# Converting weights beside a recurrence: more places for raw words, two pieces under way, fewer loads ahead of the inputs

## Chip, cores, metric

One core of one Trainium2 chip. The metric is device time in microseconds (us); the lower the better. Executions of one kernel within a round lie within about 0.5% of each other, so effects of a few tenths of a per cent need several runs and an interval; all runs here were in the fast state. Ratios are the mean time of one kernel's fast runs over that of the other's of the same rounds, so not quite the ratio of the medians that I quote. The experiments ran in other rounds than the result did: where two kernels of different rounds are compared, the ratios decide, and I give the difference that they make beside that of the medians.

## The reference, cut to what matters

```python
B, H, S, D = 4, 8, 768, 40
for t in range(S):                               # per batch and head, state is D x D
    y[:, :, t] = einsum('bhd,bhde->bhe', r_t, state)
    Sa = einsum('bhde,bhe->bhd', state, a_t)
    state = state * w_t[:, :, None, :] - outer(Sa, b_t) + outer(v_t, k_t)
x = y.transpose(0, 2, 1, 3).reshape(3072, 320)
h = x @ w_in                                     # 320 x 2048
out = (h * clip(h + 3, 0, 6) / 6) @ w_out        # 2048 x 320
```

The two weight matrices arrive as 64-bit floats. The kernel loads them as pairs of 32-bit words and makes 32-bit floats of them with its own operations, in 20 pieces of 512 KB.

## The kernel before

The recurrence is computed in blocks of 64 time steps. 24 units (a block of two batch entries' heads) are handled in groups of four. For each group a triangular matrix is inverted on VectorE (`fb` is its first operation, `tb` and `tt` its last two); a "third block" then completes the inverse with two small products on TensorE. Inverse and inputs feed the recurrence step of each unit (`U`, `UT`, `score`, `state`, `yg`), whose result `xt` feeds the two large products with `win` and `wout`.

The weight conversion is a Python generator. Each `next(weights)` puts one step of it into the instruction streams, between other work. In these traces each engine takes up its operations in the order of the program (in e1 below, VectorE stands in front of one of them until 46.09 us, and all that follows comes later), so where a step stands in the program decides what it can hold up.

```python
def raw_homes():             # where a piece's raw words land, and which piece must be done first
    ...                      # a, b: half of a free buffer each; c, d: in wout; e, f: in win
    order = [a, b, c, d, e, f, a, b, c, d, a, b, c, d, a, b, None, None, a, b]
    free = [None] * 6 + [0, 1, 2, 3, 6, 7, 8, 9, 10, 11, None, None, 14, 15]   # None: fb, tt

for _ in range(4):           # four loads at once, on SP's queue, ahead of V and of the next inputs
    load()
yield
while n < PIECES + 2:        # three pieces under way (begun, not finished): n, n-1, n-2
    # piece n:    exponent:  VectorE shift/and -> parts, then ScalarE scales parts     | step
    # piece n-1:  sign:      VectorE or's the sign into parts                          | step
    #             mantissa:  VectorE and/or on raw, then ScalarE scales raw            | step
    # piece n-2:  combine:   VectorE raw = lo * 2**-52 + raw                           | step
    #             product:   VectorE out = raw * parts; done; load what may be loaded  | step
```

```python
for t, _ in enumerate(by_twos(0, 4, MIXED, 0, {5: 1, 6: 1, 10: 1})):   # prepare 4 units
    ...                      # conversion steps at t = 5, 6 and 10: six by then
while not third:             # the inversion: one conversion step for every third of its steps
    ...
while phase[0] in (3, 4):    # finish the piece's combine and product
    next(weights)
firsts = [third_block(*third[-1], n, True) for n in (0, 2)]
run(firsts[0])
next(firsts[1])              # the second block's first product, sent ahead
run(firsts[0], weight=1)
...
for t in range(LAST + OWN):  # the first group's recurrence, 2.5 conversion steps a TensorE stage
    if t in (1, 3): run(firsts[1])
    ...
```

```python
def third_block(F, tb, tt, n, others=False):
    ...                                            # 32 small products into zp
    for x in range(2): nc.scalar.activation(out=zs[...], in_=zp[x][...])      # 32x512 each
    if others:
        for z in range(0, P, BL):
            nc.scalar.activation(out=tinv[z:z + L, heads, 0:L], in_=tb[...])
            nc.gpsimd.tensor_copy(tinv[z + L:z + BL, heads, L:BL], tb[...])
    ...                                            # 32 small products into tp
    for x in range(2): nc.scalar.activation(out=tinv[..., L:BL], in_=tp[x][...])
```

## Time and profile before

| | before |
|---|---|
| time, median | 864.86 us (864.53 to 865.4, 4 runs) |
| span of the profiled run | 863.8 us, mean TensorE clock 0.926 |
| TensorE busy | 781 us, 90% of the span |
| VectorE busy | 530 us, 61% |
| ScalarE, GpSimd busy | 312 us, 150 us |

The lines behind this are in the prediction below. TensorE is full from about 160 us on. Everything that the change touches lies before that. So I follow a few marks through all the kernels: the start of `fb` (the inversion may begin), the start of `tb` (it ends), the first U product (the recurrence begins), and the first scan of the second group (`prods`, after which only work follows that no kernel here changes, save the last conversions).

### The profile page before, as it was taken

The page shows a single profiled execution, that of the slowest core. Times are in us where ns is not written, and L with a number is a line of the kernel's source. Part 1 is how long each engine was busy: PE and PEld are TensorE (multiplying, and loading weights), DVE is VectorE, ACT ScalarE, POOL GpSimd, SP SyncE. Part 2 cuts the span into 40 slices and gives each one's busy share as a digit, 9 for nine tenths or more (in the row PEclk, how much of TensorE's full clock was granted, in tenths as well). Part 3 has the DMA queues.
Part 4 walks back from the last instruction along what each step waited for, and adds up shares of the span by engine and source line. Part 5 has one row for each costly group of instructions (what it writes and reads, how often), then busy time and mean ns, then how long its engine had stood idle before and what let it go on. Part 6 is the DMA issues. An engine that isn't in the chain of part 4 may idle for free.

```text
span 863.8 us, 34857 instructions
## 1 busy us (share of the span) xinstructions
PE 781.1 (90%) x15480; PEld 668.2 (77%) x15480; DVE 529.6 (61%) x1032; ACT 311.9 (36%) x752; POOL 150.2 (17%) x295
## 2 busy tenths in 40 slices
PE   4541787898999999999999999999999999999998
PEld 3441766687888787888888888888888888888886
DVE  6689777967954669845589643698445774221211
ACT  1223744232344443344423534325453324222211
POOL 4220210122112130311130222112112201000000
PEclk8565657898999998999999999999999999999999
DMA  7733263431033331322321333222132101100000
GB/s 150 147 69 88 52 163 84 79 56 34 16 57 55 55 60 27 55 44 41 54 49 31 58 55 52 41 51 37 37 60 43 26 18 27 28 20 14 15 19 16
DMA packets 174326, 45.00 MB, mean 52 GB/s; under 512 B 157408, under 2 KB 172768, under 8 KB 174176
## 3 DMA queue, kind: packets, MB, share of 16 engines
q1 hardware_dynamic: 165632, 41.46, 24.9%
q10 hardware_dynamic: 8544, 1.31, 1.0%
q8 instruction: 122, 2.00, 1.0%
q14 instruction: 28, 0.23, 0.1%
HBM read 34.08 MB, written 3.93 MB: 44 GB/s over the span
## 4 chain that ended last, share of the span: by engine, by line
PE 77%; DVE 10%; DMA 5%; issue 3%; SPq 2%; ACT 1%; POOL 1%; ACTq 0%; DVEq 0%
PE o L936 24%; PE h L912 20%; PE any L418 6%; PE h L917 6%; PE any L436 3%; PE any L809 3%; PE any L832 3%; PE any L656 2%; SPq L404 2%; DVE prod L624 2%; DVE x L630 2%; DMA raw<-in_moe_w_in_dram 1%; PE any L716 1%; PE any L754 1%; PE any L581 1%
## 5 line engine op out<-in xcount | busy, mean ns | idle before, releaser
L936 PE MATMUL o<-wout,gt 128*128 128x320 f32 x768 | 232.5, 449 | 0.0
L912 PE MATMUL h<-xt,win 128*128 128x128 f32 x1536 | 197.3, 283 | 3.7 <-DVE gt L923 3.7
L912 PEld LDWEIGHTS h<-xt,win 128*128 128x128 f32 x1536 | 186.0, 196 | 11.7 <-DVE gt L923 3.8
L936 PEld LDWEIGHTS o<-wout,gt 128*128 128x128 f32 x768 | 141.2, 192 | 55.7 <-issue 2.4
L923 DVE SCALAR_TENSOR_TENSOR gt<-gt,h 128x512 f32<-128x512 f32 x96 | 61.3, 679 | 98.2 <-ACT gt L922 98.1
L922 ACT ACTIVATE gt<-h,three 128x512 f32<-128x512 f32 x96 | 60.6, 683 | 132.4 <-PE h L917 128.7
L847 POOL TENSOR_TENSOR yg<-ys,gam 128x512 f32<-128x512 f32 x24 | 41.7, 1736 | 234.8 <-DVE ys L844 123.0
L624 DVE TENSOR_TENSOR prod<-x 128x30 f32<-128x30 f32 (+9 forms) x180 | 65.6, 365 | 13.6 <-POOL x L615 8.1
L630 DVE TENSOR_TENSOR x<-x,prod 128x30 f32<-128x30 f32 (+9 forms) x180 | 64.5, 358 | 5.7 <-DMA R<-in_r_dram 0.4
L554 POOL TENSOR_TENSOR KBt<-K,rgt 128x320 f32<-128x320 f32 x24 | 21.6, 898 | 211.2 <-ACT rgt L546 211.2
L917 PE MATMUL h<-xt,win 64*128 64x128 f32 x768 | 55.8, 285 | 0.0
L445 DVE COPY_PREDICATED score<-mask,any 128x256 f32<-128x256 int32 x143 | 53.0, 433 | 3.2 <-PE any L436 3.2
L917 PEld LDWEIGHTS h<-xt,win 64*128 64x128 f32 x768 | 46.6, 187 | 4.5 <-issue 0.3
L472 DVE RECIPROCAL gam<-prods 128x256 f32<-128x256 f32 x24 | 41.4, 1740 | 13.5 <-POOL yg L847 13.2
L844 DVE TENSOR_TENSOR ys<-any,ys 128x256 f32<-128x256 f32 x44 | 16.6, 418 | 49.6 <-PE any L581 32.4
L487 DVE RECIPROCAL rgam<-prods 128x256 f32<-128x256 f32 x24 | 41.8, 1740 | 0.0
L461 DVE TENSOR_TENSOR_SCAN prods<-wm,start 128x528 f32<-128x528 f32 x24 | 30.0, 1252 | 17.0 <-ACT wm L458 15.4
L695 ACT ACTIVATE RT<-any 128x512 f32<-128x512 f32 x24 | 14.3, 595 | 71.6 <-PE any L418 71.5
L816 DVE TENSOR_TENSOR state<-any,state 128x160 f32<-128x160 f32 x48 | 13.2, 315 | 44.0 <-PE any L436 40.1
L587 ACT ACTIVATE EV<-any 64x160 f32<-64x160 f32 x92 | 24.8, 295 | 36.2 <-PE any L581 22.0
L832 PE MATMUL any<-score,KBt 64*64 64x64 f32 x1536 | 30.2, 229 | 1.7 <-DVE RR L721 1.4
L832 PEld LDWEIGHTS any<-score,KBt 64*64 64x64 f32 x1536 | 26.6, 142 | 6.5 <-issue 3.7
(159 smaller groups left out, 1144.1 us busy)
## 6 DMA issues: line engine op xcount, KB each, us to landing
V<-in_v_dram SPq DMA_DIRECT2D x96, 40.0 KB
out_dram<-ob SPq DMA_DIRECT2D x48, 80.0 KB
B<-in_b_dram SPq DMA_DIRECT2D x46, 80.0 KB
K<-in_k_dram SPq DMA_DIRECT2D x46, 80.0 KB
R<-in_r_dram SPq DMA_DIRECT2D x84, 40.0 KB
W<-in_w_dram SPq DMA_DIRECT2D x40, 80.0 KB
A<-in_a_dram SPq DMA_DIRECT2D x40, 80.0 KB
raw<-in_moe_w_out_dram SPq DMA_DIRECT2D x6, 512.0 KB
```

Of the source, the lines that this page charges most:

```text
L418: nc.tensor.transpose(out=o[:, n, :], in_=x[:, 2 * n:2 * n + 2, :].rearrange("p s e -> p (s e)"), identity=ident[:])
L445: nc.vector.copy_predicated(out=x[:, 4 * i:4 * i + 4, :], mask=mask4, data=o[i])
L487: nc.vector.reciprocal(rv[:, :, HB:BL], o["prods"][:, :, 1, 1:HB + 1])
L624: nc.vector.tensor_tensor(out=pv, in0=_ap(x[:], (i + 1) * L + i, [[L, n], [0, i]]), in1=_ap(x[:], i * L, [[0, n], [1, i]]), op=ALU.mult,)
L630: nc.vector.tensor_tensor(out=rest, in0=rest, in1=pv, op=ALU.add)
L832: nc.tensor.matmul(out=y[q][half(s), pr, :], lhsT=o[name][half(q), h * D:h * D + SLOT], rhs=m[name][half(q), 4 * rs + 2 * s + j, :], start ...
L847: nc.gpsimd.tensor_tensor(out=yg[:], in0=m["ys"][:].rearrange("p r q t -> p r (q t)"), in1=o["G"][:], op=ALU.mult)
L912: nc.tensor.matmul(out=hp[c][:, i, :], lhsT=win[:, t, j * P:(j + 1) * P], rhs=xt[:, t, :], start=(t == 0 and i == 0), stop=False)
L917: nc.tensor.matmul(out=hp[c][:, i, :], lhsT=win2[half(c), (j0 + i) * P:(j0 + i + 1) * P], rhs=xt[half(c), 2, :], start=False, stop=(i == N ...
L922: nc.scalar.activation(out=gt[:], in_=hp[c][:], func=AF.Relu, bias=three[:], scale=1.0)
L923: nc.vector.scalar_tensor_tensor(out=gt[:], in0=gt[:], scalar=6.0, in1=hp[c][:], op0=ALU.min, op1=ALU.mult)
L936: nc.tensor.matmul(out=op[:], lhsT=gts[c][:, n, :], rhs=wout[:, c * HJ + r * NQ + n, :], start=((split or r == 0) and c == 0 and n == 0), ...
```

## The change

Its intent: let inputs pass ahead of weights at the start; let weight loads run further ahead later, by three more places; give a place back sooner by having two pieces under way; let the first unit's recurrence begin when its own half of the inverse is there.

```diff
-        order = [a, b, c, d, e, f, a, b, c, d, a, b, c, d, a, b, None, None, a, b]
-        free = [None] * 6 + [0, 1, 2, 3, 6, 7, 8, 9, 10, 11, None, None, 14, 15]
+        order = [a, b, c, d, e, f, a, b, c, d, a, b, "fb", "tt", "x", d, a, b, "fb", "tt"]
+        free = [None] * 6 + [0, 1, 2, 3, 6, 7, None, None, None, 9, 10, 11, 12, 13]
...                                                   # load(): stops at limit[0], 2 at first
-        for _ in range(4):
-            load()
+        while load():
+            pass
...                                                   # the loop, two pieces under way:
-        # n: exponent | n-1: sign | n-1: mantissa | n-2: combine | n-2: product
+        # n: exponent | n-1: combine | n-1: product | n: sign | n: mantissa
...                                                   # in the preparation's loop:
+        limit[0] = {7: 4, 10: 12}.get(t, limit[0])
+        while t == 7 and refill[0]():
+            pass
...
-    while phase[0] in (3, 4):
+    while phase[0] in (1, 2, 3):
...
-    next(firsts[1])
...                                                   # in the recurrence's loop:
+        if t == 3:
+            limit[0] = PIECES
...                                                   # third_block, for the first blocks:
+        parts = [slice(0, H), slice(H, 2 * H)] if first else [slice(0, 2 * H)]
...          # every copy once per part; tb's copies on ScalarE go to GpSimd
```

More of the change, by code (lines that the diff above doesn't have):

```diff
@@ L224 @@
     phase = [0]
+    limit, refill = [2], []
     def raw_homes():
@@ L238, in raw_homes @@
         a, b, c, d, e, f = places
-        order = [a, b, c, d, e, f, a, b, c, d, a, b, c, d, a, b, None, None, a, b]
-        free = [None] * 6 + [0, 1, 2, 3, 6, 7, 8, 9, 10, 11, None, None, 14, 15]
+        order = [a, b, c, d, e, f, a, b, c, d, a, b, "fb", "tt", "x", d, a, b, "fb", "tt"]
+        free = [None] * 6 + [0, 1, 2, 3, 6, 7, None, None, None, 9, 10, 11, 12, 13]
+        left = {}
         for n, (x, before) in enumerate(zip(order, free)):
-            if x is None:
-                x = inv.tile([P, L, L], F32, name=f"raw{n}", tag=("fb", "tt")[n % 2])
-                x = x[:].rearrange("p t s -> p (t s)").bitcast(U32)
+            if isinstance(x, str):
+                if x not in left:
+                    left[x] = inv.tile([P, L, L], F32, name=f"raw_{x}", tag=x)
+                x = left[x][:].rearrange("p t s -> p (t s)").bitcast(U32)
                 x = x.rearrange("p (n c t) -> p n c t", n=2, t=2)
@@ L258, in load @@
         def load():
+            if issued[0] == min(PIECES, limit[0]):
+                return False
             if not upcoming:
-                if issued[0] == PIECES:
-                    return False
                 upcoming.append(next(homes))
@@ L272, in load @@
             return True
-        for _ in range(4):
-            load()
+        while load():
+            pass
+        refill.append(load)
         phase[0] = 0
         yield
-        stages = deque([None, None])
-        n = 0
-        while n < PIECES + 2:
+        before = None
+        for n in range(PIECES + 1):
             now = None
             if n < PIECES:
-                if not loaded:
-                    load()
+                while load():
+                    pass
                 out, raw = loaded.popleft()
+                hi = raw[:, :, :, 1]
                 x = ffn.tile([P, 2, WC], U32, name="parts", tag="gt", bufs=5)
-                now = n, out, raw, x
-                nc.vector.tensor_scalar(x[:], raw[:, :, :, 1], 20, 0x7FF, ALU.logical_shift_right,
+                now = out, raw, x
+                nc.vector.tensor_scalar(x[:], hi, 20, 0x7FF, ALU.logical_shift_right,
                                         ALU.bitwise_and)
                 nc.scalar.activation(out=x[:], in_=x[:], func=AF.Relu, bias=low[:], scale=2.0 ** 23)
-                if n < 2:
-                    load()
                 phase[0] = 1
                 yield
-            stages.append(now)
-            if stages[1]:
-                _, out, raw, x = stages[1]
-                hi = raw[:, :, :, 1]
+            if before:
+                out, raw, y = before
+                m, yf = raw[:, :, :, 1].bitcast(F32), y[:].bitcast(F32)
+                nc.vector.scalar_tensor_tensor(m, raw[:, :, :, 0], 2.0 ** -52, m, ALU.mult, ALU.add)
+                phase[0] = 2
+                yield
+                if len(out.shape) == 4:
+                    m, yf = (z.rearrange("p n (j c) -> p n j c", c=out.shape[3]) for z in (m, yf))
+                nc.vector.tensor_tensor(out=out, in0=m, in1=yf, op=ALU.mult)
+                converted[0] += 1
+                done.append(n - 1)
+                while load():
+                    pass
+                phase[0] = 3
+                yield
+            if now:
                 nc.vector.scalar_tensor_tensor(x[:], hi, 0x80000000, x[:], ALU.bitwise_and,
                                                ALU.bitwise_or)
-                phase[0] = 2
+                phase[0] = 4
                 yield
@@ L305, in load_weights @@
                                         ALU.bitwise_or)
-                hi = hi.bitcast(F32)
-                nc.scalar.activation(out=hi, in_=hi, func=AF.Copy, bias=-7.0, scale=2.0 ** -20)
-                phase[0] = 3
-                yield
-            if stages[0]:
-                k, out, raw, x = stages[0]
-                hi = raw[:, :, :, 1].bitcast(F32)
-                nc.vector.scalar_tensor_tensor(hi, raw[:, :, :, 0], 2.0 ** -52, hi, ALU.mult, ALU.add)
-                phase[0] = 4
-                yield
-                m, xf = hi, x[:].bitcast(F32)
-                if len(out.shape) == 3 and out.shape[1] != 2:
-                    m, xf = (y.rearrange("p n (j c) -> p (n j) c", c=out.shape[2]) for y in (m, xf))
-                elif len(out.shape) == 4:
-                    m, xf = (y.rearrange("p n (j c) -> p n j c", c=out.shape[3]) for y in (m, xf))
-                nc.vector.tensor_tensor(out=out, in0=m, in1=xf, op=ALU.mult)
-                converted[0] += 1
-                done.append(k)
-                while load():
-                    pass
+                m = hi.bitcast(F32)
+                nc.scalar.activation(out=m, in_=m, func=AF.Copy, bias=-7.0, scale=2.0 ** -20)
                 phase[0] = 5
                 yield
-            stages.popleft()
-            n += 1
+            before = now
     def weight_pieces():
@@ L647, in invert, with third_block @@
         yield
-    def third_block(F, tb, tt, n, others=False):
-        heads = slice(n * H, (n + 2) * H)
+    def third_block(F, tb, tt, n, first=False):
         zs = tmp.tile([P, 2 * H, L], F32, name="zs")
+        parts = [slice(0, H), slice(H, 2 * H)] if first else [slice(0, 2 * H)]
         zp = [ps_any([P, 2 * H, L]) for _ in range(2)]
@@ L659, in third_block @@
         yield PE
-        for x in range(2):
-            z = x * BL
-            nc.scalar.activation(out=zs[z:z + L], in_=zp[x][z:z + L], func=AF.Copy)
-        if others:
-            for z in range(0, P, BL):
-                nc.scalar.activation(out=tinv[z:z + L, heads, 0:L], in_=tb[z:z + L, heads],
-                                     func=AF.Copy)
-                nc.gpsimd.tensor_copy(tinv[z + L:z + BL, heads, L:BL], tb[z + L:z + BL, heads])
+        for part in parts:
+            for x in range(2):
+                z = x * BL
+                nc.scalar.activation(out=zs[z:z + L, part], in_=zp[x][z:z + L, part], func=AF.Copy)
+        if first:
+            for part in parts:
+                heads = slice(n * H + part.start, n * H + part.stop)
+                for z in range(0, P, BL):
+                    nc.gpsimd.tensor_copy(tinv[z:z + L, heads, 0:L], tb[z:z + L, heads])
+                    nc.gpsimd.tensor_copy(tinv[z + L:z + BL, heads, L:BL], tb[z + L:z + BL, heads])
         yield DONE
@@ L676, in third_block @@
         yield PE
-        for x in range(2):
-            z = x * BL
-            nc.scalar.activation(out=tinv[z:z + L, heads, L:BL], in_=tp[x][z:z + L], func=AF.Copy)
+        for part in parts:
+            heads = slice(n * H + part.start, n * H + part.stop)
+            for x in range(2):
+                z = x * BL
+                nc.scalar.activation(out=tinv[z:z + L, heads, L:BL], in_=tp[x][z:z + L, part],
+                                     func=AF.Copy)
         yield DONE
@@ L1040 @@
             next(weights)
+        limit[0] = {7: 4, 10: 12}.get(t, limit[0])
+        while t == 7 and refill[0]():
+            pass
         if t == RFETCH:
```

## The prediction

> **What bounds the kernel now.** I read four views, in this order: the page's slices, the waits of VectorE from 0 to 48 us with the timeline there, the waits of VectorE from 87 to 160 us, and the chain of work that ended last. The slices show where there is still time to gain.
>
> ```profile
> PE   4541787898999999999999999999999999999998
> ...
> DVE  6689777967954669845589643698445774221211
> ...
> PEclk8565657898999998999999999999999999999999
> DMA  7733263431033331322321333222132101100000
> ```
>
> A slice is 21.6 us. From the eighth or ninth on (about 160 us) TensorE is at 8 or 9 tenths and its clock near full: from there a fixed amount of matmul work sets the end. Only before that are there large gaps, and there the whole diff acts. So I take it that the end moves by what the start gets shorter, and ask what sets the start. It has three stretches: **A**, four units are prepared until their inversion can begin (0 to 47 us); **B**, the inversion on VectorE with weight conversions between its steps (47 to 87 us); **C**, the first recurrence steps with the rest of the conversions (87 to about 155 us, the last conversion ends at 155.5).
>
> Stretch A: VectorE's waits (total us, times, longest us), then two lines of the timeline.
>
> ```profile
> DVE bt L496 <- PE h L418: 6.5, 2, 3.6
> ...
> DVE fb L612 <- ACT F L516: 1.3, 1, 1.3
> ```
> ```profile
> 37.34 1.08 PE L418 MATMUL h<-ident,B 128*128 128x128 f32 x4 [2.42 <-DMA B<-in_b_dram]
> ...
> 41.62 1.09 PE L418 MATMUL h<-ident,B 128*128 128x128 f32 x4 [3.20 <-DMA B<-in_b_dram]
> ```
>
> VectorE waits 6.5 us for two transposes, and the transposes wait for the B input of the third and fourth unit. VectorE is otherwise busy nearly all the time from 14 us to 35.6 us. So the inputs of the second pair come late by 6.5 us, and then B begins (fb, 47.35 us). The next view says why they are late: the order of issue on the SP queue.
>
> ```profile
> 13.22 2.02 SPq L270 DMA_DIRECT2D raw<-in_moe_w_in_dram  x4
> 15.28 1.82 SPq L270 DMA_DIRECT2D wout<-in_moe_w_in_dram  x4
> 18.18 8.33 SPq L401 DMA_DIRECT2D V<-in_v_dram  x8
> ...
> 30.66 2.04 SPq L270 DMA_DIRECT2D win<-in_moe_w_in_dram  x4
> 32.81 1.28 SPq L404 DMA_DIRECT2D B<-in_b_dram  x2
> ...
> 36.21 1.14 SPq L270 DMA_DIRECT2D win<-in_moe_w_out_dram  x2
> 37.44 1.28 SPq L404 DMA_DIRECT2D B<-in_b_dram  x2
> ```
>
> Six weight pieces of 512 KB are issued before the second B. V's eight issues took 8.33 us here and 5.25 us at 40 us, so the queue also pushed back behind the weights.
>
> Stretch C: VectorE's waits from 87 to 160 us, and what the chain that ended last has there (start us, us, what).
>
> ```profile
> DVE parts L288 <- DMA raw<-in_moe_w_in_dram: 3.6, 2, 2.1
> DVE parts L288 <- DMA raw<-in_moe_w_out_dram: 3.1, 2, 2.4
> ...
> DVE parts L288 <- DMA wout<-in_moe_w_in_dram: 1.4, 1, 1.4
> ```
> ```profile
> 100.28 5.16 DMA raw<-in_moe_w_in_dram
> ...
> 109.63 4.45 DMA wout<-in_moe_w_in_dram
> ...
> 119.48 2.77 DMA raw<-in_moe_w_in_dram
> ...
> 122.51 5.09 DMA raw<-in_moe_w_out_dram
> ...
> 135.61 3.94 DMA raw<-in_moe_w_out_dram
> ```
>
> The chain goes through five weight loads, 21.4 us together; VectorE stands still for 8.1 us of that, and since it works in program order, the recurrence's own operations stand behind it. The loop is: a piece is done, its place is free, the next load starts, four to five us later the load lands, the conversion that was already due goes on.
>
> **What the Trainium skill says.** "DMA: Bandwidth & Descriptors", section "Issuing engines are not separate DMA queues": all issuers share the same 16 DMA engines and interleave. The trace agrees: 79% DMA share from 20 to 40 us, and V slowed behind weights. The same page, "Rules for kernel authors": issue a DMA early and wait for it late, so that its cost lies beside compute. The five loads above break that, with up to 5.2 us each from issue to landing on the chain. "GPSIMD Engine Reference", "Engine selection": one-input elementwise work runs about at line rate there. Here the 32x512 copies (L667) took 605 to 1043 ns on GpSimd and 627 ns on ScalarE (L665): agreement at best, worse beside VectorE. "TensorE: Matmul & The Clock Gate", "What's actually happening": recent activity releases the clock. The trace agrees in sense: 0.50 to 0.62 from 60 to 140 us, 1.00 in most of what follows 160 us.
>
> **The change part by part.**
>
> 1. *Fewer loads ahead of the inputs.* The limit is 2 pieces until step 7 of the preparation, so four of the six pieces leave the queue ahead of the second B. Issue time saved: 1.82 + 2.04 + 1.14 = 5.0 us, and V's push-back, 8.33 - 5.25 = 3.1 us if it all goes. The second B's issue moves from 37.4 to about 30 us, the first's to the moment its buffer is free (KBt's copies end at 27.4 and 29.1 us). Landing 4.2 to 4.5 us after issue as now, they are there at 32 and 34 to 35 us, before VectorE is through with its own work at 35.6. The 6.5 us go. Cost: the first sign operation now follows its own exponent directly, with ScalarE's 0.72 us between; the wait of 0.5 us there becomes about 1.0. And before the inversion two conversion operations of 0.68 replace 0.42 + 0.68, but a ScalarE operation of 0.72 ahead of F's copies goes. Sum for A: 6.5 - 0.5 + 0.5, so **6.5 us** sooner.
>
> 2. *Stretch B.* The number of conversion steps between inversion steps is unchanged, and so are their operations (0.42, 0.68, 0.42, 0.68, 0.68 us a piece). Piece 2 is now first read at the ninth step instead of the fifth, about 8 us into B; its load, issued near 40 us, should be there. **0 us.**
>
> 3. *More places, two pieces under way.* Counting conversion steps in the code (five a piece, 2.5 per TensorE stage in C): piece k was done at step 5k+9 and is done at 5k+6; piece n was first read at step 5n-5 and is at 5n-1. What matters is the distance from a place's release to the read of the piece loaded into it. Before, from piece 10 on, the place came from piece n-4 (save 16 and 17): 5n-11 to 5n-5, six steps, a little over one piece's time, and with SP's own issues ahead of it the load of 4 to 5 us is not covered. Afterwards pieces 12 to 14 take places that no conversion has to release (fb, tt, x, free once the first third blocks are through), the later ones come from piece n-6: 5n-24 to 5n-1, 23 steps. Pieces 10 and 11 keep n-4, but now that is 13 steps. So all five chain loads leave the chain. No VectorE operation is added. VectorE's 8.1 us of waiting are the direct worth. Its whole idle time from 87 to 155 us is some 15 us, 3.9 of it on the state's matmuls and 2.4 on gt, which stay. In place of the DMA the recurrence's own TensorE and ScalarE waits should take a little: I count 85% of 8.1, **7 us**. The conversions fall as exponent with combine, then product, sign and mantissa, 2.5 steps per TensorE stage, so ScalarE's results have a stage between them and their reader; I charge nothing for the shorter pipeline.
>
> 4. *Third blocks by unit.* Two ScalarE copies of tb (1.27 us) per block go to GpSimd, in eight halves, at an estimated 0.4 to 0.6 us each; they need only tb (ready 87.1) and so end about 91.5, ahead of the last product. zs and the last copies are halved: four of about 0.37 in place of two of 0.59. The product can begin after two of them, the first unit's U after two more: about 0.4 us at each of two places, **1 us**.
>
> Sum 6.5 + 0 + 7 + 1 = 14.5 us. I take off 10% for what is lost on the way to the end, 13 us: **852 us**.
>
> **The rivals.**
>
> *The recurrence takes over in C.* TensorE's own waits from 87 to 160 us are for state (3.9 us), gt (3.7) and ScalarE (about 4). If the weights only hid these, the 7 become 2 and the time is 857. Against it: the chain stays with the conversions and their loads nearly without a break from 98 to 140 us.
>
> *The loads collide later.* About 2 MB move from before 40 us to after it, onto V, A and R of the second pair. If piece 2 or the last inputs come late, B begins its conversions with a stall, some 2 to 4 us: 855. For it: 92 GB/s are moved there already. Against it: the first DMA waits of the conversions come only after 100 us.
>
> *A warmer clock pays more.* With no DMA stalls in C TensorE is denser, and its clock may rise before 150 us. TensorE's 42 us of busy time from 87 to 140 at 0.5 to 0.7 would shrink; a part of it on the chain gives 3 to 5 us more: 847 to 849.
>
> *Nothing arrives at the end.* If the later gaps were spare time that absorbs a shift, the time stays near 862. Against it: after 160 us TensorE waits about 7 us in total up to 220 us, and none of that is for the weights.
>
> **Range and chances.** The first two rivals together make 857 to 858, the third 846 to 848. Range 846 to 858. Two per cent faster means under 847.8, which needs the third rival or the whole of C's idle time: 0.22. Slower by two per cent has no mechanism: 0.01.
>
> **What would show it.** In the profile after: no TensorE wait on B near 40 us, and fb beginning near 41 us instead of 47.35 (step 1); tb 38 us after fb, as now (step 2); no VectorE wait of parts on a weight DMA between 87 and 155 us, the chain free of weight loads, and the last product about 14 us earlier, near 141 (step 3); the first U about 5 us after tb's end instead of 6 (step 4). The prediction is wrong if fb does not move, if the DMA waits turn into waits of parts or raw on ScalarE, or if the last product comes 14 us sooner and the end does not.

## The result

| | before | after |
|---|---|---|
| time, median | 864.86 us | 860.60 us (859.18 to 860.94, 4 runs) |
| ratio | | 0.9947, 95% interval 0.993 to 0.9964 |
| span of the profiled run | 863.8 us | 859.2 us |
| TensorE / VectorE busy | 781.1 / 529.6 us | 779.3 / 531.6 us |

Faster by 0.5%, where 1.5% was forecast. The marks tell where it went (us; from one profile each. The changed kernel, e7, e8 and e10 below have the same program up to `fb` and begin it between 39.93 and 40.66, so up to 0.7 us is noise):

| mark | before | after | lead | forecast lead |
|---|---|---|---|---|
| fb begins | 47.35 | 39.93 | 7.4 | 6.5 |
| tb begins | 85.20 | 78.40 | 6.8 | 6.5 |
| first U product | 93.18 | 85.58 | 7.6 | 7.5 |
| first scan, second group | 155.42 | 149.25 | 6.2 | 14.5 |
| end | 863.8 | 859.2 | 4.6 | 13 |

Up to the first U the forecast holds. Then the lead was to double, and it shrank. The page's slices of the changed kernel:

```profile
PE   4723877898999989999999999999999999999998
...
PEclk8755667998999999999999999999999999999999
DMA  7571452331123230322222233222132101100000
```

TensorE's slices two to six differ from those before; from the seventh on it is nearly the old picture. The SP queue of the changed kernel (start us, us, instruction), to be held against the seven lines of before:

```profile
13.22 2.03 SPq L273 DMA_DIRECT2D raw<-in_moe_w_in_dram  x4
15.29 6.68 SPq L396 DMA_DIRECT2D V<-in_v_dram  x8
...
27.04 2.06 SPq L399 DMA_DIRECT2D B<-in_b_dram  x2
...
30.57 1.27 SPq L399 DMA_DIRECT2D B<-in_b_dram  x2
```

Two weight pieces in place of six stand ahead of the second B, which is issued at 30.6 instead of 37.4 us. VectorE's wait of 6.5 us for `bt` is gone; its work then runs without a gap into `fb` at 39.93. A wait of 1.3 us of `fb` on ScalarE's copies of F went too, since the conversion's operation ahead of them did. This part did what it was meant to do.

Now VectorE's waits of the changed kernel from 87 to 160 us (total us, times, longest us):

```profile
DVE parts L313 <- ACT parts L294: 5.3, 3, 2.2
DVE raw L300 <- ACT raw L321: 2.7, 3, 1.9
DVE prods L456 <- ACT wm L453: 2.6, 2, 1.8
...
DVE raw_fb L300 <- ACT raw_fb L321: 0.8, 2, 0.4
...
DVE wout L300 <- ACT wout L321: 0.4, 1, 0.4
```

No wait for a weight load is left in this view, where there were 8.1 us. In their place stand 5.3 + 2.7 + 0.8 + 0.4 = 9.2 us in which VectorE waits for ScalarE's two conversion operations, and before there were none. (Counted from its own tb, 78.40 us, one more such wait belongs to the changed kernel, 1.9 us at 84.67 us: 11.1 us in all.) One new wait took the place of another. The largest single one, on both engines' timelines:

```profile
103.05 0.60 ACTq L396 DMA_DIRECT2D R<-in_r_dram  x1
103.61 0.57 ACT L697 ACTIVATE RT<-any 128x512 f32<-128x512 f32 x1
103.69 3.24 ACTq L396 DMA_DIRECT2D R<-in_r_dram  x3
106.98 0.72 ACT L294 ACTIVATE parts<-parts,low 128x512 uint32<-128x512 uint32 x1 [2.79 <-DMA raw_x<-in_moe_w_in_dram]
```
```profile
103.32 0.42 DVE L292 TENSOR_SCALAR parts<-raw 128x512 uint32<-128x512 uint32 x1
...
107.73 0.69 DVE L313 SCALAR_TENSOR_TENSOR parts<-raw,parts 128x512 uint32<-128x512 uint32 x1 [2.23 <-ACT parts L294]
```

VectorE had the exponent ready at 103.74. ScalarE came to it at 106.98, since it stood in its own queue's four issues of R from 103.05 to 106.93 (one operation, RT, ran beside the first). The bracket in ScalarE's line blames the load of `raw_x` for 2.79 us, but VectorE reads that piece only at 119.67 us; e7 will test the queue. It was held while the weights were being loaded at the same time (82% DMA share and 204 GB/s moved from 100 to 113 us). VectorE, with only combine and product between the exponent and the sign, then waited. In the kernel before, the same four issues held ScalarE from 109.62 to 112.34 us, and its list has no wait of `parts` or `raw` on ScalarE.

So the theory that I took into the experiments: **with two pieces under way VectorE has no slack against a ScalarE that is held by something else.** The rival is the prediction's own: the recurrence's chain takes over once the loads are gone, whatever the pipeline.

### The profile page after: what moved, and what is told of

Same layout as the page of the kernel before. It is cut to its first block, busy times and chain, and to the rows that moved or that the text cites. A ratio compares the mean times of both kernels' runs of the same rounds, so it can differ in the third digit from the quotient of the medians.

```text
span 859.2 us, 34883 instructions
## 1 busy us (share of the span) xinstructions
PE 779.3 (91%) x15480; PEld 665.8 (77%) x15480; DVE 531.6 (62%) x1032; ACT 311.3 (36%) x756; POOL 157.3 (18%) x307
## 4 chain that ended last, share of the span: by engine, by line
PE 75%; DVE 14%; issue 3%; ACT 3%; DMA 3%; SPq 2%; POOL 0%; ACTq 0%; DVEq 0%
PE o L938 23%; PE h L914 19%; PE any L413 6%; PE h L919 5%; PE any L431 3%; PE any L811 3%; DVE x L625 2%; DVE prod L619 2%; PE any L834 2%; PE any L653 2%; PE any L672 2%; PE any L756 1%; SPq L399 1%; PE any L576 1%; PE any L718 1%
## 5 line engine op out<-in xcount | busy, mean ns | idle before, releaser
L619 DVE TENSOR_TENSOR prod<-x 128x30 f32<-128x30 f32 (+9 forms) x180 | 65.7, 365 | 13.6 <-POOL x L610 8.1
```

The costliest lines, as they stand in the source:

```text
L619: nc.vector.tensor_tensor(out=pv, in0=_ap(x[:], (i + 1) * L + i, [[L, n], [0, i]]), in1=_ap(x[:], i * L, [[0, n], [1, i]]), op=ALU.mult,)
```

## The experiments

"C" is the length from tb to the first scan, "tail" from that scan to the end of the span, both from each run's profile. Times are medians, ratios against the kernel before in the same rounds.

| run | time us | ratio (95%) | fb | C | tail |
|---|---|---|---|---|---|
| before | 864.86 | | 47.35 | 70.2 | 708.4 |
| after | 860.60 | 0.9947 (0.993 to 0.9964) | 39.93 | 70.9 | 710.0 |
| e1 inputs first alone | 867.12 | 1.0022 (1.0015 to 1.003) | 48.39 | 71.7 | 708.9 |
| e2 places alone | 859.69 | 0.994 (0.9927 to 0.9952) | 47.18 | 65.1 | 707.8 |
| e3 third blocks alone | 865.85 | 1.0011 (1.0002 to 1.0019) | 46.77 | 71.4 | 708.0 |
| e4 after, three pieces | 863.47 | 0.9978 (0.997 to 0.9986) | 48.82 | 65.8 | 709.0 |
| e5 e4, loads after step 5 | 855.21 | 0.9889 (0.9874 to 0.9904) | 41.26 | 66.7 | 708.4 |
| e6 e5, old third blocks | 854.13 | 0.9876 (0.9862 to 0.989) | 40.85 | 65.7 | 707.9 |
| e7 after, issues off ScalarE | 856.71 | 0.9908 (0.9895 to 0.9922) | 40.38 | 66.7 | 710.3 |
| e8 after, one piece ahead | 859.05 | 0.9936 (0.9923 to 0.9948) | 40.66 | 69.3 | 708.5 |
| e9 e6, issues off ScalarE | 853.61 | 0.9865 (0.9847 to 0.9884) | 40.82 | 65.6 | 708.5 |
| e10 e7 and e8 | 856.21 | 0.989 (0.9873 to 0.9907) | 40.22 | 67.0 | 708.1 |

### First four: each part alone, and the pipeline undone

**e1**, in the kernel before: `limit` and `refill` as in the change, with {7: 4, 10: PIECES}; nothing else.

> The kernel before with one part alone: two weight pieces ahead of the inputs, two more after step 7, the rest from step 10; places, three pieces under way and third blocks as before. Theory (the inputs' gain is whole and reaches the end): fb begins near 40 us instead of 47.35, the first U near 86, and the time is 7 us under before, 857 to 858.5. Rival (the moved loads come back as waits in the conversions after 87 us): fb as early, but the DMA waits of parts grow from 8.1 to 11 us or more and the time is 861 to 863.

Both theories failed: 867.12 us, slower than before. `fb` came no sooner (48.39 us). Its VectorE waits from 0 to 48 us say why:

```profile
DVE parts L290 <- DMA wout<-in_moe_w_in_dram: 8.4, 1, 8.4
```

The inputs did come early. But with three pieces under way, piece 2 is read at the fifth conversion step, which stands in the program ahead of `fb`. Its load was now issued after step 7 of the preparation, at 40.5 us. VectorE sat in front of that one operation until 46.09, and everything behind it, `fb` included, came later than in the kernel before. In the change the same load is harmless because two pieces under way put that read off to the ninth step, behind `fb`. So as it is written, the first part of the change pays only together with the two pieces under way.

**e2**, in the kernel before:

```diff
-        order = [..., a, b, c, d, a, b, None, None, a, b]
+        order = [..., a, b, "fb", "tt", "x", d, a, b, "fb", "tt"]     # and free, as in the change
+    limit = [12] until t == 3 of the recurrence                       # fb, tt are free from there
```

> The kernel before with one part alone: the new order of places (fb, tt, x for pieces 12 to 14), three pieces under way, four loads ahead as before. Theory (weight loads set stretch C, and what ate the gain is the shorter pipeline): the DMA waits of parts from 87 to 160 us fall from 8.1 to under 3 us and the time falls by 4 to 7 us, 858 to 861. Rival (the recurrence's own chain sets stretch C, the loads only hid it): the DMA waits fall as much, waits on other engines take their place, and the time stays within 1.5 us of before.

859.69 us, as the theory had it, and about what the whole change brings (the intervals overlap). C is 5.1 us shorter. The waits of VectorE from 87 to 160 us, where before has 8.1 us on weight loads:

```profile
DVE parts L291 <- DMA raw<-in_moe_w_in_dram: 1.1, 1, 1.1
...
DVE parts L291 <- DMA raw_fb<-in_moe_w_out_dram: 0.2, 1, 0.2
```

6.8 us of waiting removed, 5.1 us of C gained: a quarter is lost to something else, and that is the most that the prediction's rival can claim. What takes that quarter was not tested.

**e3**, in the kernel before: `third_block` as in the change, `next(firsts[1])` taken out.

> The kernel before with one part alone: third blocks copied by unit, tb's copies on GpSimd, the second block's first product no longer sent ahead. Theory (in the changed kernel the lead on before fell from 7.6 us at the first U to 5.1 us at the first score after it, where the second block's product now stands among the recurrence): the first U comes 0.5 to 1 us sooner, the first score 1 to 2 us later, the time is 1 to 2 us over before. Rival (the prediction's): 1 us under before.

865.85 us, 0.1% slower. From tb's start the first U comes after 7.2 us instead of 8.0, the gain that I forecast at 1 us. But the first score after it comes 16.7 us after tb instead of 15.0, and C as a whole is 1.2 us longer. The second block's first product now stands among the recurrence's own stages; that this is the cause is likely, not shown, since e3 changes the copies as well.

**e4**, in the changed kernel: the loop of the kernel before, `while phase[0] in (3, 4)`.

> The changed kernel with three pieces under way again, all else as changed. Theory (VectorE's 9.2 us of waits on ScalarE's parts and raw from 87 to 160 us are what the shorter pipeline costs): those waits fall under 3 us and the time falls 3 to 6 us, to 855 to 858. Rival (the recurrence's own chain takes over whatever the pipeline): the waits fall but the time stays within 1.5 us of the changed kernel's 860.6.

863.47 us, slower than the changed kernel, so both stated ranges failed, and the reason is that of e1: its wait of `parts` on `wout` before `fb` is 8.3 us, and `fb` comes at 48.82. But C, the stretch in dispute, is 65.8 us against 70.9: 5.0 us shorter with three pieces, and VectorE waits for ScalarE's `parts` or `raw` nowhere in it. The theory was right for C, and I had not thought of what three pieces do before `fb`.

### Second four: getting both gains

**e5**, in e4:

```diff
-        limit[0] = {7: 4, 10: 12}.get(t, limit[0])
-        while t == 7 and refill[0]():
+        limit[0] = {5: 4, 10: 12}.get(t, limit[0])
+        while t == 5 and refill[0]():
```

> The changed kernel with three pieces under way, and pieces 2 and 3 loaded after step 5 of the preparation instead of step 7, that is directly behind the inputs of the second pair. Theory (the inputs' gain was lost in e1 and e4 only because, with three pieces, piece 2 is read before fb and its load stood behind V; it is a matter of that one load): the 8.3 us wait of parts on wout falls under 1 us, fb begins near 40 us, stretch C keeps e4's length, and the time is 7 to 9 us under e4's 863.5, 854 to 857. Rival (two pieces are needed for the inputs' gain, the load comes too late in any place after the inputs): the wait stays at 4 us or more, the time is 859 to 861.

855.21 us. The loads of pieces 2 and 3 now stand directly behind the second pair's inputs and ahead of V. The 8.3 us became

```profile
DVE parts L292 <- DMA wout<-in_moe_w_in_dram: 0.5, 1, 0.5
```

and `fb` begins at 41.26, with C still short: 66.7 us, 4.2 under the changed kernel. As e5 starts as early as that kernel does and e4 does not, 4.2 us is the fairer price of two pieces in C. They are not needed for the inputs' gain.

**e6**, in e5: `third_block` and `next(firsts[1])` as before the change.

> e5 with the third blocks as before the change, so the kernel before with only inputs first, places and the load after step 5. Theory (third blocks by unit cost about 1 us, as e3 says): 1 us under e5, 853 to 856, which beats both kernels by 4 us or more. Rival (they gain once C is not held by loads): 1 us over e5.

854.13 us, 1.1 us under e5, so third blocks by unit cost about a microsecond here too, with the loads out of the way (the intervals of e5 and e6 overlap; e3's lies wholly above 1, and both point the same way). This version keeps two of the change's four parts, with one load moved, and beats both kernels: 1.2% under before, 0.7% under after.

**e7**, in the changed kernel:

```diff
-            fetch("R", i + 1, nc.scalar if i < NU - 1 else None)
+            fetch("R", i + 1)                       # SP's queue
...
-                fetch(name, NU + 1, nc.scalar)      # W, A of unit 5
+                fetch(name, NU + 1)
```

> The changed kernel with R of units 1 to 3 and W and A of unit 5 issued from SP instead of ScalarE's queue. Theory (with two pieces under way VectorE waits for ScalarE because ScalarE's own DMA issues hold it, 3.8 us near 103 and 3.7 us near 131): the waits of parts and raw on ScalarE from 87 to 160 us fall from 9.2 to about 5 us and the time falls 3 to 4 us, to 857. Rival (it is the short distance itself, one VectorE operation between ScalarE's copy and its reader): the waits fall by under 1.5 us, the time stays within 1 us of 860.6 or grows because R comes later.

856.71 us: the theory's number (3.9 us by the medians, 3.4 by the ratios; the intervals are apart). The first of VectorE's waits after 87 us is cut from 5.3 us to

```profile
DVE parts L313 <- ACT parts L294: 1.2, 1, 1.2
```

while `raw` on ScalarE stays at 2.7; all waits on ScalarE's conversions from 87 to 160 us fall from 9.2 to 5.1 us. C is 66.7 us, 4.1 shorter, the same as that of e5. No operation changed, only the queue from which five small groups of input loads are issued. So of the 4.2 to 5.0 us that two pieces cost in C (against e5 or e4), 4.1 go with the DMA issues that hold ScalarE.

**e8**, in the changed kernel: five more `next(weights)`, one piece, ahead of the third blocks.

> The changed kernel with five more conversion steps (one whole piece) taken before the third blocks, so that the last piece does not end behind the second group's first scan. Theory (after that scan the changed kernel loses 1.6 us against before because the last two conversion operations stand between the scan and the reciprocals): the last product ends before the first scan, and the time falls 1.5 to 3 us, to 858. Rival (the five steps delay the first U by what they save): within 0.7 us of 860.6.

859.05 us, 1.5 us less by the medians, 1.0 by the ratios, whose intervals overlap: on the clock the gain is not shown. It tests the last loss, between the scan and the end. The changed kernel's VectorE there:

```profile
149.25 1.26 DVE L456 TENSOR_TENSOR_SCAN prods<-wm,start 128x528 f32<-128x528 f32 x1 [1.82 <-ACT wm L453]
151.30 1.29 DVE L456 TENSOR_TENSOR_SCAN prods<-wm,start 128x528 f32<-128x528 f32 x1 [0.79 <-ACT wm L453]
152.51 0.66 DVE L300 SCALAR_TENSOR_TENSOR raw_tt<-raw_tt 128x512 f32<-128x512 uint32 x1
153.21 0.78 DVE L305 TENSOR_TENSOR wout<-raw_tt,parts 128x512 f32<-128x512 f32 x1
153.91 3.35 DVE L467 RECIPROCAL gam<-prods 128x256 f32<-128x256 f32 x2
```

The last piece's combine and product stand between the second scan and the reciprocals that the second group needs. In the kernel before they were done ahead of the first scan:

```profile
154.81 0.69 DVE L321 TENSOR_TENSOR wout<-raw,parts 128x512 f32<-128x512 f32 x1
155.42 1.25 DVE L461 TENSOR_TENSOR_SCAN prods<-wm,start 128x528 f32<-128x528 f32 x1
157.46 1.26 DVE L461 TENSOR_TENSOR_SCAN prods<-wm,start 128x528 f32<-128x528 f32 x1 [0.79 <-ACT wm L458]
158.63 3.34 DVE L472 RECIPROCAL gam<-prods 128x256 f32<-128x256 f32 x2
```

This follows from the change of `phase`: the kernel before takes two extra conversion steps ahead of the third blocks (29 in all), the changed one takes none (27), so its conversion ends two steps later in the program. From the second scan to the reciprocals it is 2.61 us in the changed kernel and 1.17 before. With e8 the tail is 708.5 us again, 1.4 shorter. The two kernels with the late last piece (the changed one and e7) have tails of 710.0 and 710.3 us, the other ten 707.8 to 709.0. C is 1.5 shorter as well, with 3.5 us of waits of `parts` on ScalarE in place of 5.3, although the first U comes 2.7 us later than in the changed kernel (88.26); so e8's time alone does not measure the tail.

### Last two: does each explanation hold where it should not act?

**e9**, in e6: the edit of e7.

> e6 with R of units 1 to 3 and W and A of unit 5 issued from SP, the edit of e7 on the version with three pieces under way. Theory (three pieces have slack enough that a ScalarE held by its DMA issues costs little; only two pieces turn the hold into a VectorE wait): the time falls by at most 1.5 us from e6's 854.1, to 852.6 or more. Rival (the hold costs the recurrence 3 to 4 us whatever the pipeline, and e7's gain says nothing about two pieces): 850 to 851.

853.61 us. Where the edit gave 3.9 us with two pieces (3.4 by the ratios), it gives 0.5 with three (1.0), and C is the same to 0.1 us. The difference of e9 and e6 is within the intervals. Nor was ScalarE held less with three pieces. In e5, which differs from the changed kernel only in the loop with three pieces and the earlier load, its own timeline has

```profile
104.87 3.15 ACTq L405 DMA_DIRECT2D R<-in_r_dram  x3
108.06 0.69 ACT L311 ACTIVATE raw<-raw 128x512 f32<-128x512 f32 x1 [2.69 <-DMA raw_x<-in_moe_w_in_dram]
```

and VectorE waits for ScalarE's `parts` or `raw` nowhere from 80 to 160 us. This ties the hold of ScalarE to the pipeline: with a piece more under way the hold is absorbed.

**e10**, in the changed kernel: the edits of e7 and e8.

> The changed kernel with the edits of e7 and e8 together. Theory (the two losses, the held ScalarE and the last piece behind the scan, are separate): 3.9 + 1.5 = 5.4 us under 860.6, about 855.2. Rival (the same wait counted twice): 856.7 as e7.

856.21 us by its median, ratio 0.989 against e7's 0.9908. The median is close to the rival's number and the ratio is nearer the theory's; the intervals overlap. In the profile the tail is 708.1 against e7's 710.3, and C is 0.3 longer. Whether the two gains add in full stays open.

## Why the prediction was wrong, point by point

What the runs show for the changed kernel, each from a difference of marks above, against the steps of the prediction (us, minus is faster). The three terms of C are steps on one way from before to after, so their sum closes by construction and proves none of them; other pairs of runs give the values in brackets:

| term | forecast | shown | from |
|---|---|---|---|
| inputs first, up to fb | -6.5 | -7.4 | after against before |
| stretch B, fb to tb | 0 | +0.6 | after against before |
| places, in C | -7 | -5.1 | e2 against before |
| third blocks by unit | -1 | +0.7 | e4 against e2 (e5 against e6: +0.9; e3: +1.2) |
| two pieces under way, in C | 0 | +5.0 | after against e4 (against e5: +4.2) |
| two conversion steps behind the scan | 0 | +1.6 | tails of after and before (timeline: +1.4) |
| sum | -14.5 | -4.6 | span: -4.6 |

1. *Fewer loads ahead of the inputs: right in mechanism and size.* The issue moved to 30.6 us, the wait on B went, `fb` came at 39.93 (forecast: near 41). What I did not see is that it depends on two pieces under way. I wrote that piece 2 is read at the ninth step instead of the fifth, and saw in it only a read that should find its load there; e1 and e4 show that, with the load after step 7, it is what makes the gain possible.

2. *Stretch B: right*, 38.5 us against 37.9.

3. *Places and two pieces: this is the step that failed.* The part on places was right: the waits on loads went, for 5.1 us rather than 7 (e2). Its last sentence was wrong: "ScalarE's results have a stage between them and their reader; I charge nothing for the shorter pipeline." I had counted TensorE stages between conversion steps. Most stages put nothing on VectorE, so on that engine the steps follow each other directly, and what stands between ScalarE's result and its reader is one VectorE operation for the mantissa and two for the exponent. In the kernel before it was five for both. The short distance alone shows as waits of about 0.4 us each. The large ones come when ScalarE is held, by its DMA issues (e7: 4.1 us of C), and, by the timeline only, by the third blocks' copies (`raw` waited 1.9 us near 91 us, behind four copies of `zs`). The term was 0 in my sum and measured +4.2 to +5.0. The prediction did name this as one of the signs that would show it wrong. Another came with it: the last product ended at 154.0 us, 1.5 us earlier than before instead of 14.

4. *Third blocks: wrong in sign.* The first U came sooner by the amount that I forecast (7.2 us after tb for 8.0), and that was not what counted: C as a whole grew by 0.7 to 1.2 us. The product no longer sent ahead is the likely reason (e3's timeline); no run has it alone.

5. *What I left out:* the two steps that end up behind the scan, 1.4 us by the timeline and 1.6 by the tails. It was in the diff, in one changed tuple of phases.

6. *The range.* The first two rivals were added wrongly: 5 us for the recurrence and 2 to 4 for the collision, on 852, make 859 to 861, not 857 to 858, and the third was put at 847 to 849 in one place and at 846 to 848 in another. With the right sum the range would have reached 860.6, but by luck: the first accounts for at most a quarter of the loads' worth, the second did not happen as described, and what cost the most, ScalarE's results coming late, is in neither.

Two readings of the trace in the prediction show less than it says. V and the weights before it were both issued by SP, so V's delay is no test of what the skill says about several issuers. And VectorE was busy beside the fast GpSimd copies too (its transpose of `tt` runs from 86.98 to 88.95 us, two copies from 87.25 to 88.52), so only some of its operations slow them.

Of the rivals, "the recurrence takes over" is true for a quarter of the loads' worth at most (e2). "The loads collide later" did not happen in B: the first read of piece 2 waited 0.4 us. But the burst of loads at 98 to 109 us did, by the timeline, fall together with R's issue. "A warmer clock" paid nothing that shows: from tb to the first scan the granted clock rose from 0.62 to 0.67 and TensorE's busy time fell from 54.2 to 52.9 us, but the stretch did not get shorter. "Nothing arrives at the end" is wrong: the tail is constant to 1.2 us in all kernels but the two with the late last piece.

Open: whether the gains of e7 and e8 add in full, what takes the quarter of e2's gain, and what the 5.1 us of waits on ScalarE that e7 leaves are worth (its C is already that of e5, which has none).

## What to carry to other kernels

A pipeline between two in-order engines should be judged by what stands between a result and its reader on the reading engine itself, and by the longest time for which the writing engine can be held by anything else, its own DMA issues included; one piece fewer under way brought nothing here that a load moved by two steps did not bring too, and cost 4.2 to 5.0 us. When a load is moved behind something urgent, look for the first instruction that reads it and what stands behind that instruction in its stream: one operation on piece 2 cost e1 and e4 the whole gain of 7 us, and moving its load by two steps of the program gave it back. Try the parts of a combined change alone: two of the four, with that load moved, were worth 1.2%, all four 0.5%.

## What the Trainium skill lacked or had wrong

- "DMA: Bandwidth & Descriptors", section "Issuing engines are not separate DMA queues", says that issuing from several engines only saves sequencer time, "usually small relative to the DMA itself". The section gives no size for what that time costs the compute that stands behind the issues on the same engine. Here four issues of 40 KB each took from 103.05 to 106.93 us while weights were loaded from SP, ScalarE sat idle behind them for 2.8 us, and moving such issues to SP brought 3.4 us by the ratios, 3.9 by the medians (e7).
- No page that I used says how much slack a pipeline across two in-order engines needs. The runs: 4.2 to 5.0 us for one piece less of it over 15 pieces (after against e5 and e4), next to nothing for the same hold with three pieces (e9: C the same to 0.1 us).
